# Attention decode with K turned as 32-bit words, column-tiled scores and PV, and fp32 selection matmuls for the outputs

## The chip, the cores and the metric

The kernel runs on one core of a Trainium2 chip. The metric is the device time of that core in microseconds. The profiler's "span" (first to last instruction) is about 1.75 us shorter than that time. TensorE is called PE, VectorE DVE, ScalarE ACT, and the queue that issues the loads SP. A run is called slow when it is over 1.5% above the fastest of the same kernel. A median is over all runs of a kernel, of which one of the changed kernel (127.4 us) and one of a3 (131.91 us) were slow.

## The reference

One decode step for a batch of 8, with attention (32 query heads, 8 key/value heads, a window of 1024 of 4096 positions, head size 128) and a gated feed-forward block beside it.

```python
xn = layernorm(x)                                   # 8 x 512
q  = (xn @ wq)                                      # wq 512 x 4096
k, v = repeat(k_cache[:, :, -1024:, :], 4), repeat(v_cache[:, :, -1024:, :], 4)
p  = softmax(q @ k.T * 128 ** -0.5)
s  = (p @ v).reshape(8, 1, 4096) @ wo               # wo 4096 x 512
g  = silu((gelu(xn @ w_gate) * (xn @ w_up)) @ w_down)   # 512 x 1792, 1792 x 512
out = x + s * g
```

47.46 MB (millions of bytes) have to be read once. In units of 1024 x 1024 bytes, K and V are 32 of it, wq and wo 8, and the feed-forward weights 5.3. Little is computed with each byte.

## The kernel before

The work is cut into 16 groups, each one batch element and four of the eight key/value heads. A group has 1 MB of K and 1 MB of V, one load each. In a K tile partition (n, p) holds 32 positions of head n, each 128 numbers long. PE turns K in 32 pieces of 128 x 128 bf16, DVE copies the turned pieces out of PSUM, 32 small matmuls give the scores (a first product puts -30000 where query and key head differ), ACT takes the exponential, one product with ones gives the row sums, and 32 small matmuls give the outputs.

```python
def load_wq(k):
    t = slot()
    nc.sync.dma_start(out=t, in_=A_wq[k * P : (k + 1) * P, :])
    return t

def turn_k(g, t):                                   # t = 0..3, eight pieces each
    kp = ps_t.tile([P, 8 * P], BF16, name="t_ps")
    for c in range(8):
        r = 8 * t + c
        nc.tensor.transpose(kp[:, c * P : (c + 1) * P], k_t[g][:, r * Dh : (r + 1) * Dh], ident)
    kT = kT_pool.tile([P, 8 * P], BF16, name="kT")
    nc.vector.tensor_copy(out=kT, in_=kp)
    ...
# score(g, t): the mask product (hot x far), then eight 128x128 kT pieces by 16 columns of q
# soft(g): Exp;  values(g): ones x p, 32 pieces of V by 16 columns of p, reduce, reciprocal, multiply

for g in range(NGR + 1):
    ...                                             # issue the loads of V[g], K[g + 2]; at the end the weights
    # turn_k(g, 0..3) interleaved with score(g, 0..2); values(g - 1); score(g, 3); soft(g)
hT = ffn_up()
ffn_down(hT)
...                                                 # 64 products with wo, then s * g + x
```

The softmax here doesn't subtract the row's maximum and nothing guards it: scores larger than these inputs give would overflow.

## Time and profile before

| | before |
|---|---|
| time | 123.04 us, median of three runs (123.03 to 123.2) |
| read from HBM | 47.46 MB |
| PE instructions (matmuls and weight loads) | 1772 + 1772 |
| PE per group at full clock | 4.44 us |
| K and V of a group arrive in | 4.9 us |
| attention ends | 98.5 us |
| last wo load complete | 117.45 us |
| from there to the end of the span | 3.85 us |

From the page of before: busy tenths of the engines in 40 slices of the span, PE's granted clock in tenths, the DMA engines' share and rate, and from the table of DMA queues the instruction fetches (packets, MB, share of 16 engines).

```profile
span 121.3 us, 3885 instructions
PE 96.0 (79%) x1772; PEld 75.6 (62%) x1772; DVE 73.6 (61%) x142; ACT 14.9 (12%) x24; POOL 3.1 (3%) x8
...
PEclk9999955555799999999999999555799955555798
DMA  2999999999999999999999999999999999999820
GB/s 78 394 430 427 427 432 430 416 413 430 424 432 421 430 427 424 408 419 427 432 421 427 419 432 419 421 421 432 430 416 419 419 437 414 416 422 417 343 86 3
...
q8 instruction: 14, 0.23, 0.7%
```

The DMA row is at 9 from the second slice to the 37th: the stream never rests. The last three slices are its ragged end. The windows view of before shows the same; the columns are the stretch in us, its length, busy time (and instructions) of each engine, PE's clock, DMA share and GB/s.

```profile
18.00:24.00 6.00, 6.00 (x85) 4.74 (x83) 3.44 (x6) 1.39 (x2) 0.00 (x0) 0.50 1.02 427
...
114.00:116.00 2.00, 1.09 (x18) 0.87 (x16) 0.00 (x0) 0.00 (x0) 0.00 (x0) 1.00 0.52 207
116.00:118.00 2.00, 1.28 (x17) 0.85 (x15) 0.15 (x1) 0.00 (x0) 0.00 (x0) 1.00 0.20 70
```

The chain of waits of before (start in us, length in us, what it was), first one group of attention in mid-stream, then the end.

```profile
40.99 0.91 PE t_ps L230 x16
41.90 0.32 PE sc_ps L242
...
44.20 0.23 PE a_ps L273
44.43 0.79 PE o_ps L282 x32
...
45.43 0.60 PE t_ps L230 x8
...
101.12 16.03 DMA slot<-in_A_wo_dram
117.15 0.04 issue
117.19 0.64 PE big L469 x8
```

One group takes 45.43 - 40.99 = 4.44 us, half a microsecond less than its data need to arrive, so PE waits for data from 54 us on. Sixteen bf16 transposes take 0.91 us, 57 ns each. At the end PE waits for the last two wo loads (landing at 117.15 and 117.45 us) and has eight products left (L469).

### The profile page before, as it was taken

How to read it: one execution, taken by the hardware profiler on the slowest of the kernel's cores; microseconds unless marked ns; L12 is line 12 of the kernel's file. 1: busy time of each engine (PE TensorE's matmuls, PEld its weight loads, DVE VectorE, ACT ScalarE, POOL GpSimd, SP SyncE). 2: the span in 40 equal slices, each digit the busy share in tenths (PEclk: the TensorE clock that was granted, in tenths of full speed). 3: DMA queues.
4: the chain of work that ended last, by engine and by line, in shares of the span. 5: the costliest groups of instructions: out<-in, count | busy, mean ns of one | idle time of the engine just before them, and what ended most of it. 6: DMA issues, size and time to landing. Idle time of an engine off the chain costs nothing.

```text
span 121.3 us, 3885 instructions
## 1 busy us (share of the span) xinstructions
PE 96.0 (79%) x1772; PEld 75.6 (62%) x1772; DVE 73.6 (61%) x142; ACT 14.9 (12%) x24; POOL 3.1 (3%) x8
## 2 busy tenths in 40 slices
PE   0197269999999999999799993999999783396660
PEld 0192028897787887887778873897888550064540
DVE  4663035475888887888688882665788644704011
ACT  4000043010101101101101101010101103002000
POOL 7200000000000000000000000000000000000000
PEclk9999955555799999999999999555799955555798
DMA  2999999999999999999999999999999999999820
GB/s 78 394 430 427 427 432 430 416 413 430 424 432 421 430 427 424 408 419 427 432 421 427 419 432 419 421 421 432 430 416 419 419 437 414 416 422 417 343 86 3
DMA packets 7392, 47.72 MB, mean 393 GB/s; under 512 B 808, under 2 KB 976, under 8 KB 2768
## 3 DMA queue, kind: packets, MB, share of 16 engines
q1 hardware_dynamic: 7312, 47.46, 93.6%
q8 instruction: 14, 0.23, 0.7%
q10 hardware_dynamic: 64, 0.02, 0.1%
q14 instruction: 2, 0.02, 0.0%
HBM read 47.46 MB, written 0.01 MB: 391 GB/s over the span
## 4 chain that ended last, share of the span: by engine, by line
DMA 56%; PE 34%; DVE 4%; SPq 2%; issue 1%; DVEq 0%
DMA slot<-in_A_k_cache_dram 17%; DMA slot<-in_B_w_up_dram 15%; PE t_ps L230 15%; DMA slot<-in_A_wo_dram 13%; DMA slot<-in_A_wq_dram 10%; PE sc_ps L253 7%; PE o_ps L282 5%; PE sc_ps L242 3%; DVE kT L234 3%; PE a_ps L273 2%; SPq L84 1%; PE t_ps L345 1%; DVE q_sb L340 1%; SPq L89 1%; PE big L469 1%
## 5 line engine op out<-in xcount | busy, mean ns | idle before, releaser
L234 DVE COPY kT<-t_ps 128x1024 bf16<-128x1024 bf16 x64 | 42.6, 690 | 17.4 <-PE t_ps L230 16.6
L230 PE MATMUL t_ps<-ident,slot 128*128 128x128 bf16 x512 | 43.7, 244 | 2.8 <-DMA slot<-in_A_k_cache_dram 2.8
L230 PEld LDWEIGHTS <-slot 128*128 128x128 bf16 x512 | 35.2, 110 | 3.3 <-DMA slot<-in_A_k_cache_dram 3.0
L253 PEld LDWEIGHTS <-kT 128*128 128x128 bf16 x512 | 18.6, 99 | 9.0 <-DVE kT L234 7.3
L253 PE MATMUL sc_ps<-qT_all,kT 128*128 128x16 bf16 x512 | 22.7, 172 | 1.8
L266 ACT ACTIVATE p<-sc_ps 128x512 bf16<-128x512 f32 x16 | 9.6, 597 | 68.1 <-PE sc_ps L253 68.1
L282 PEld LDWEIGHTS <-slot 128*128 128x128 bf16 x512 | 15.7, 98 | 3.5 <-issue 2.2
L282 PE MATMUL o_ps<-p,slot 128*128 128x16 bf16 x512 | 15.7, 171 | 0.0
L290 DVE TENSOR_REDUCE sums<-a_ps 128x16 f32<-128x512 f32 x16 | 11.1, 692 | 1.4 <-PE a_ps L273 1.0
L469 PE MATMUL big<-slot,og 128*64 128x256 bf16 x64 | 5.8, 332 | 2.8 <-DMA slot<-in_A_wo_dram 2.8
L273 PE MATMUL a_ps<-p,ones_pp 128*128 128x512 bf16 x16 | 7.1, 442 | 0.7 <-ACT p L266 0.7
L242 PE MATMUL sc_ps<-far,hot 4*128 4x512 bf16 x16 | 7.3, 453 | 0.0
L469 PEld LDWEIGHTS <-og 128*64 128x64 bf16 x64 | 4.5, 135 | 4.3 <-issue 2.8
L330 PE MATMUL big<-slot,xT 128*32 128x512 bf16 x32 | 3.4, 516 | 3.9 <-DMA slot<-in_A_wq_dram 3.9
L362 PE MATMUL big<-slot,xT 128*32 128x448 bf16 x32 | 3.6, 566 | 2.0 <-DMA slot<-in_B_w_up_dram 2.0
L294 DVE TENSOR_TENSOR oT_all<-o_ps,sums 128x16 bf16<-128x16 f32 x16 | 3.7, 230 | 1.7
L404 PE MATMUL big<-slot,hT 128*32 128x256 bf16 x28 | 3.3, 415 | 1.7 <-DVE hT L389 1.7
L330 PEld LDWEIGHTS <-xT 128*32 128x32 bf16 x32 | 0.9, 104 | 5.8 <-issue 5.7
L340 DVE CAST q_sb<-big 128x512 bf16<-128x512 f32 x1 | 0.7, 692 | 6.2 <-PE big L330 6.2
L293 DVE RECIPROCAL sums<-sums 128x16 f32<-128x16 f32 x16 | 4.0, 253 | 0.5
L480 DVE TENSOR_TENSOR tmp<-big,g_sb 128x256 f32<-128x256 f32 x1 | 0.4, 425 | 6.2 <-PE big L469 6.2
L404 PEld LDWEIGHTS <-hT 128*32 128x32 bf16 x28 | 2.1, 138 | 3.3 <-DVE hT L389 2.5
(50 smaller groups left out, 28.5 us busy)
## 6 DMA issues: line engine op xcount, KB each, us to landing
slot<-in_A_k_cache_dram SPq DMA_DIRECT2D x16, 1024.0 KB, 19.7
slot<-in_A_v_cache_dram SPq DMA_DIRECT2D x16, 1024.0 KB, 20.3
slot<-in_A_wq_dram SPq DMA_DIRECT2D x4, 1024.0 KB, 9.7
slot<-in_A_wo_dram SPq DMA_DIRECT2D x3, 1024.0 KB, 17.7
slot<-in_B_w_gate_dram SPq DMA_DIRECT2D x2, 896.0 KB, 19.4
slot<-in_B_w_up_dram SPq DMA_DIRECT2D x2, 896.0 KB, 18.6
slot<-in_B_w_down_dram SPq DMA_DIRECT2D x2, 896.0 KB
slot<-in_A_wo_dram SPq DMA_DIRECT2D x1, 512.0 KB
```

Of the source, the lines that this page charges most:

```text
L230: nc.tensor.transpose(kp[:, c * P : (c + 1) * P], k_t[g][:, r * Dh : (r + 1) * Dh], ident)
L234: nc.vector.tensor_copy(out=kT, in_=kp)
L242: nc.tensor.matmul(sc.rearrange("p r q -> p (r q)"), hot, far.rearrange("n r q -> n (r q)"), start=True, stop=False, skip_group_check=True,)
L253: nc.tensor.matmul(sc[:, r, :], kT_t[g, t][:, c * P : (c + 1) * P], qT_all[:, i, b, :, :].rearrange("p n j -> p (n j)"), start=False, stop ...
L266: nc.scalar.activation(out=p, in_=sc_t[g], func=ACT.Exp, scale=inv_sqrt_dh)
L273: nc.tensor.matmul(sums_ps.rearrange("p r q -> p (r q)"), ones_pp, p.rearrange("p r q -> p (r q)"), start=True, stop=True,)
L282: nc.tensor.matmul(o_ps, v_t[g][:, r * Dh : (r + 1) * Dh], p[:, r, :], start=(r == 0), stop=(r == NKR - 1),)
L290: nc.vector.tensor_reduce(out=sums, in_=sums_ps.rearrange("p r q -> p q r"), axis=AX.X, op=ALU.add)
L293: nc.vector.reciprocal(out=sums, in_=sums)
L330: nc.tensor.matmul(q_ps[i][32 * j : 32 * j + 32, :], xT[:, 0, k, :], wq_t[k][:, n0 : n0 + 512], start=(k == 0), stop=(k == NDC - 1), tile_ ...
L404: nc.tensor.matmul(f_ps[64 * t : 64 * t + 32, 0:256], hT[:, j, :], w[:, c0 : c0 + 256], start=(j == 0), stop=(j == FR - 1), tile_position= ...
L469: nc.tensor.matmul(s_ps[64 * t : 64 * t + 64, 0:256], og[:, hh, j, :], wo_t[q][:, c0 : c0 + 256], start=(n == 0), stop=(n == len(rows) - 1 ...
```

## The change

The change cuts PE's and DVE's instruction count. K is turned as 32-bit words, two bf16 numbers at a time, so 16 transposes do what 32 did; the scores are then split over even and odd numbers and run as four column tiles of N=512; PV runs as two column tiles of N=512 with P turned on DVE; and the wanted blocks of the PV result are gathered by fp32 products with a selection matrix. The last wq block, one w_down block and the last wo blocks are loaded in smaller pieces, and the residual x is loaded between the wo loads. Cut to its core:

```diff
 def load_wq(k):
     t = slot()
-    nc.sync.dma_start(out=t, in_=A_wq[k * P : (k + 1) * P, :])
+    n = 2 if k == NDC - 1 else 1
+    w = Hq * Dh // n
+    for c in range(0, Hq * Dh, w):
+        nc.sync.dma_start(out=t[:, c : c + w], in_=A_wq[k * P : (k + 1) * P, c : c + w])
 ...
 def turn_k(g, t):
-    for c in range(8):                              # bf16, 128 x 128
+    kw = k_t[g].bitcast(FP32)
+    for c in range(4):                              # words, 128 x 128
+        nc.tensor.transpose(kp[:, c * P : (c + 1) * P], kw[:, rp * P : (rp + 1) * P], ident_f)
-    nc.vector.tensor_copy(out=kT, in_=kp)
+    copy = nc.scalar.copy if t == 1 else nc.vector.tensor_copy
 ...
+    # score(g): mask, even, odd, each as four column tiles of 32 by N=512 (12 products)
+    # soft(g): Exp with row sums;  turn_p(g): 32x32 block transpose of P on DVE
+    # values(g): eight products of N=512 in two column tiles, then ACT copies o_ps to fp32 o_sb
+def gather(g):
+    nc.tensor.matmul(a_ps[:, 0, :], ones_f, ss_t[g], ...)               # fp32
+    for r in range(rep):
+        nc.tensor.matmul(a_ps[:, 1, :], o_t[g][:, r * Dh : (r + 1) * Dh], selr[:, r, :], ...)   # fp32
 ...
+    # Q: four casts (even/odd, twice) and eight copies of 64 partitions, on DVE and ACT in turn
 ...
-parts = [(0, 0, 8), (2, 0, 8), (4, 0, 8), (6, 0, 4), (7, 0, 3), (7, 3, 4)]
+parts = [(0, 0, 8), (2, 0, 8), (4, 0, 8), (6, 0, 4), (7, 0, 2), (7, 2, 3), (7, 3, 4)]
 ...
 for g in range(NGR + 1):
+    # score(g), soft(g), turn_k(g+1, 0), turn_p(g), turn_k(g+1, 1), values(g-1), turn_k(g+1, 2..3), gather(g-1)
```

More of the change, by code (lines that the diff above doesn't have):

```diff
@@ L59 @@
     persist = ctx.enter_context(tc.tile_pool(name="persist", bufs=1))
-    kT_pool = ctx.enter_context(tc.tile_pool(name="kT_pool", bufs=8))
-    p_pool = ctx.enter_context(tc.tile_pool(name="p_pool", bufs=3))
+    kT_pool = ctx.enter_context(tc.tile_pool(name="kT_pool", bufs=2))
+    p_pool = ctx.enter_context(tc.tile_pool(name="p_pool", bufs=2))
+    pT_pool = ctx.enter_context(tc.tile_pool(name="pT_pool", bufs=2))
     small = ctx.enter_context(tc.tile_pool(name="small", bufs=3))
+    o_pool = ctx.enter_context(tc.tile_pool(name="o_pool", bufs=1))
     ffn_sb = ctx.enter_context(tc.tile_pool(name="ffn_sb", bufs=1))
-    ps_t = ctx.enter_context(tc.tile_pool(name="ps_t", bufs=2, space=bass.MemoryType.PSUM))
-    ps_sc = ctx.enter_context(tc.tile_pool(name="ps_sc", bufs=2, space=bass.MemoryType.PSUM))
+    ps_t = ctx.enter_context(tc.tile_pool(name="ps_t", bufs=3, space=bass.MemoryType.PSUM))
+    ps_sc = ctx.enter_context(tc.tile_pool(name="ps_sc", bufs=1, space=bass.MemoryType.PSUM))
     ps_a = ctx.enter_context(tc.tile_pool(name="ps_a", bufs=1, space=bass.MemoryType.PSUM))
@@ L83, in load_wq @@
         t = slot()
-        nc.sync.dma_start(out=t, in_=A_wq[k * P : (k + 1) * P, :])
+        n = 2 if k == NDC - 1 else 1
+        w = Hq * Dh // n
+        for c in range(0, Hq * Dh, w):
+            nc.sync.dma_start(
+                out=t[:, c : c + w], in_=A_wq[k * P : (k + 1) * P, c : c + w]
+            )
         return t
@@ L107, in load_down @@
         n = FR // 2 * D
-        nc.sync.dma_start(
-            out=t[:, 0:n],
-            in_=B_w_down.rearrange("(p j) d -> p (j d)", j=FR)[:, h * n : (h + 1) * n],
-        )
+        rows = B_w_down.rearrange("(p j) d -> p (j d)", j=FR)
+        cut = [0, n] if h == 0 else [0, 4 * D, n]
+        for a, z in zip(cut, cut[1:]):
+            nc.sync.dma_start(out=t[:, a:z], in_=rows[:, h * n + a : h * n + z])
         return t
@@ L137 @@
     k_t[1] = load_kv(A_k_cache, *groups[1])
-    for g in range(NGR):
-        v_t[g] = None
-    stream = []
     ident = consts.tile([P, P], BF16, name="ident")
@@ L153 @@
     )
-    ones_pp = consts.tile([P, P], BF16, name="ones_pp")
-    nc.vector.memset(ones_pp, 1.0)
+    ident_f = consts.tile([P, P], FP32, name="ident_f")
+    nc.vector.tensor_copy(out=ident_f, in_=ident)
+    ones_f = consts.tile([P, P], FP32, name="ones_f")
+    nc.vector.memset(ones_f, 1.0)
     eps_sb = consts.tile([B, 1], FP32, name="eps_sb")
     nc.vector.memset(eps_sb, 1e-5)
-    hot = consts.tile([HN, P], BF16, name="hot")
+    hot = consts.tile([HN, 2, QW], BF16, name="hot")
     nc.vector.memset(hot, 0.0)
     nc.gpsimd.affine_select(
-        out=hot.rearrange("n (p m) -> n p m", m=HN),
-        in_=hot.rearrange("n (p m) -> n p m", m=HN),
+        out=hot.rearrange("n r (m j) -> n r m j", m=HN),
+        in_=hot.rearrange("n r (m j) -> n r m j", m=HN),
         compare_op=ALU.not_equal,
@@ L166 @@
         base=0,
-        pattern=[[0, P // HN], [-1, HN]],
+        pattern=[[0, 2], [-1, HN], [0, rep]],
         channel_multiplier=1,
     )
-    far = consts.tile([HN, NKR, QW], BF16, name="far")
+    far = consts.tile([HN, 512], BF16, name="far")
     nc.vector.memset(far, -30000.0)
     nc.gpsimd.affine_select(
-        out=far.rearrange("n r (m j) -> n r m j", m=HN),
-        in_=far.rearrange("n r (m j) -> n r m j", m=HN),
+        out=far.rearrange("n (c m) -> n c m", m=HN),
+        in_=far.rearrange("n (c m) -> n c m", m=HN),
         compare_op=ALU.not_equal,
@@ L177 @@
         base=0,
-        pattern=[[0, NKR], [-1, HN], [0, rep]],
+        pattern=[[0, 512 // HN], [-1, HN]],
         channel_multiplier=1,
+    )
+    selq = consts.tile([P, QW], FP32, name="selq")
+    nc.vector.tensor_reduce(
+        out=selq,
+        in_=ident.rearrange("p (m q) -> p q m", q=QW),
+        axis=AX.X,
+        op=ALU.add,
+    )
+    selr = consts.tile([P, rep, QW], FP32, name="selr")
+    nc.vector.tensor_reduce(
+        out=selr.rearrange("p r q -> p (r q)"),
+        in_=ident.rearrange("p (u c) -> p c u", u=2),
+        axis=AX.X,
+        op=ALU.add,
     )
@@ L199 @@
     )
-    for t in range(2):
-        nc.scalar.dma_start(
-            out=x_res[64 * t : 64 * t + B, :], in_=x_flat[:, t * 256 : (t + 1) * 256]
-        )
-    xT_ps = ps_t.tile([P, 2, NDC, 32], BF16, name="t_ps")
+    xT_ps = ps_t.tile([P, 2, NDC, 32], BF16, name="t_ps", tag="t")
     for k in range(NDC):
@@ L215 @@
     nc.vector.tensor_copy(out=xT, in_=xT_ps)
-    qT_all = persist.tile([P, NHALF, B, HN, rep], BF16, name="qT_all")
+    q2_all = persist.tile([P, NHALF, B, 2, 2, HN, rep], BF16, name="q2_all")
+    nc.gpsimd.memset(q2_all, 0.0)
     oT_all = persist.tile([P, NHALF, HN, rep, B], BF16, name="oT_all")
-    og = persist.tile([P, Hkv, rep, 64], BF16, name="og")
+    og = persist.tile([P, Hkv * rep + 1, 32], BF16, name="og")
     nc.vector.memset(og, 0.0)
-    kT_t = {}
-    sc_t = {}
-    def turn_k(g, t):
-        kp = ps_t.tile([P, 8 * P], BF16, name="t_ps")
-        for c in range(8):
-            r = 8 * t + c
-            nc.tensor.transpose(
-                kp[:, c * P : (c + 1) * P], k_t[g][:, r * Dh : (r + 1) * Dh], ident
-            )
-        kT = kT_pool.tile([P, 8 * P], BF16, name="kT")
-        nc.vector.tensor_copy(out=kT, in_=kp)
-        kT_t[g, t] = kT
@@ L237, in score, with turn_k @@
-    def score(g, t):
+    wp = persist.tile([P, P, 2], BF16, name="wp")
+    nc.gpsimd.memset(wp, 0.0)
+    nc.gpsimd.memset(wp[:, :, 0], 1.0)
+    wp_ps = ps_t.tile([P, 4 * P], FP32, name="t_ps", tag="t")
+    nc.tensor.transpose(
+        wp_ps[:, 0:P], wp.rearrange("p k e -> p (k e)").bitcast(FP32), ident_f
+    )
+    one = persist.tile([P, 1], FP32, name="one")
+    nc.vector.tensor_copy(out=one, in_=wp_ps.bitcast(BF16)[:, 0:1])
+    kT_t, p_t, pT_t, ss_t, o_t = {}, {}, {}, {}, {}
+    def turn_k(g, t):
+        kp = ps_t.tile([P, 4 * P], FP32, name="t_ps", tag="t")
+        kw = k_t[g].bitcast(FP32)
+        for c in range(4):
+            rp = 4 * t + c
+            nc.tensor.transpose(
+                kp[:, c * P : (c + 1) * P], kw[:, rp * P : (rp + 1) * P], ident_f
+            )
+        if t == 0:
+            kT_t[g] = kT_pool.tile([P, NKR * P], BF16, name="kT")
+        copy = nc.scalar.copy if t == 1 else nc.vector.tensor_copy
+        copy(out=kT_t[g][:, t * 8 * P : (t + 1) * 8 * P], in_=kp.bitcast(BF16))
@@ new lines, with score @@
+    sc_t = {}
+    def score(g):
+        b, i = groups[g]
+        sc = ps_sc.tile([P, 512], FP32, name="sc_ps")
+        sc_t[g] = sc
+        kT = kT_t[g].rearrange("w (r k e) -> w r k e", k=P, e=2)
+        for e in range(-1, 2):
+            for t in range(4):
+                if e < 0:
+                    lhs, rhs = hot.rearrange("n r q -> n (r q)"), far
+                else:
+                    lhs = q2_all[:, i, b, e, :, :, :].rearrange("w r n j -> w (r n j)")
+                    rhs = kT[:, :, 32 * t : 32 * t + 32, e]
+                nc.tensor.matmul(
+                    sc[32 * t : 32 * t + 32, :],
+                    lhs,
+                    rhs,
+                    start=(e < 0),
+                    stop=(e == 1),
+                    skip_group_check=True,
+                    tile_position=(0, 32 * t),
+                )
@@ new lines, in soft, with turn_p @@
+    def soft(g):
+        p = p_pool.tile([P, 512], BF16, name="p")
+        acc = small.tile([P, 1], FP32, name="acc")
+        nc.scalar.activation(
+            out=p, in_=sc_t[g], func=ACT.Exp, scale=inv_sqrt_dh, accum_out=acc
+        )
+        p_t[g] = p, acc
+    def turn_p(g):
+        p, acc = p_t[g]
+        pT = pT_pool.tile([P, 512], BF16, name="pT")
+        nc.vector.transpose(out=pT, in_=p)
+        pT_t[g] = pT
+        ss = small.tile([P, QW], FP32, name="ss")
+        nc.vector.tensor_scalar(
+            out=ss, in0=selq, scalar1=acc[:, 0:1], scalar2=None, op0=ALU.mult
+        )
+        ss_t[g] = ss
@@ new lines, in values @@
+    def values(g):
+        o_ps = ps_o.tile([P, 512], FP32, name="o_ps")
+        for m in range(NKR // 4):
+            u = m % 2
+            nc.tensor.matmul(
+                o_ps[64 * u : 64 * u + 64, :],
+                pT_t[g][:, m * 64 : (m + 1) * 64],
+                v_t[g][:, m * 512 : (m + 1) * 512],
+                start=(m < 2),
+                stop=(m >= NKR // 4 - 2),
+                skip_group_check=True,
+                tile_position=(0, 64 * u),
+            )
+        o_sb = o_pool.tile([P, 512], FP32, name="o_sb")
+        nc.scalar.copy(out=o_sb, in_=o_ps)
+        o_t[g] = o_sb
@@ L238, in score @@
+    def gather(g):
         b, i = groups[g]
-        if t == 0:
-            sc = ps_sc.tile([P, NKR, QW], FP32, name="sc_ps")
-            sc_t[g] = sc
-            nc.tensor.matmul(
-                sc.rearrange("p r q -> p (r q)"),
-                hot,
-                far.rearrange("n r q -> n (r q)"),
-                start=True,
-                stop=False,
+        a_ps = ps_a.tile([P, 2, QW], FP32, name="a_ps", tag="a")
+        nc.tensor.matmul(
+            a_ps[:, 0, :], ones_f, ss_t[g], start=True, stop=True, skip_group_check=True
+        )
+        for r in range(rep):
+            nc.tensor.matmul(
+                a_ps[:, 1, :],
+                o_t[g][:, r * Dh : (r + 1) * Dh],
+                selr[:, r, :],
+                start=(r == 0),
+                stop=(r == rep - 1),
@@ L248, in score @@
                 skip_group_check=True,
             )
-        sc = sc_t[g]
-        for c in range(8):
-            r = 8 * t + c
-            nc.tensor.matmul(
-                sc[:, r, :],
-                kT_t[g, t][:, c * P : (c + 1) * P],
-                qT_all[:, i, b, :, :].rearrange("p n j -> p (n j)"),
-                start=False,
-                stop=True,
-                skip_group_check=True,
-            )
-    p_t = {}
-    def soft(g):
-        p = p_pool.tile([P, NKR, QW], BF16, name="p")
-        nc.scalar.activation(out=p, in_=sc_t[g], func=ACT.Exp, scale=inv_sqrt_dh)
-        p_t[g] = p
@@ L269, in values @@
-    def values(g):
-        b, i = groups[g]
-        p = p_t[g]
-        sums_ps = ps_a.tile([P, NKR, QW], FP32, name="a_ps")
-        nc.tensor.matmul(
-            sums_ps.rearrange("p r q -> p (r q)"),
-            ones_pp,
-            p.rearrange("p r q -> p (r q)"),
-            start=True,
-            stop=True,
-        )
-        o_ps = ps_o.tile([P, QW], FP32, name="o_ps")
-        for r in range(NKR):
-            nc.tensor.matmul(
-                o_ps,
-                v_t[g][:, r * Dh : (r + 1) * Dh],
-                p[:, r, :],
-                start=(r == 0),
-                stop=(r == NKR - 1),
-            )
-        sums = small.tile([P, QW], FP32, name="sums")
-        nc.vector.tensor_reduce(
-            out=sums, in_=sums_ps.rearrange("p r q -> p q r"), axis=AX.X, op=ALU.add
-        )
-        nc.vector.reciprocal(out=sums, in_=sums)
+        rs = small.tile([P, QW], FP32, name="rs")
@@ L294, in values @@
+        nc.vector.reciprocal(out=rs, in_=a_ps[:, 0, :])
         nc.vector.tensor_tensor(
             out=oT_all[:, i, :, :, b],
-            in0=o_ps.rearrange("p (n j) -> p n j", n=HN),
-            in1=sums.rearrange("p (n j) -> p n j", n=HN),
+            in0=a_ps[:, 1, :].rearrange("p (n j) -> p n j", n=HN),
+            in1=rs.rearrange("p (n j) -> p n j", n=HN),
             op=ALU.mult,
@@ L301, in regroup @@
     def regroup(i):
-        rg = ps_a.tile([P, rep, HN, B], FP32, name="a_ps")
+        rg = ps_a.tile([P, rep, HN, B], FP32, name="rg_ps", tag="a")
         sel = ident.rearrange("p (e j) -> p j e", j=rep)
@@ L316, in regroup @@
         nc.vector.tensor_copy(
-            out=og[:, i * HN : (i + 1) * HN, :, 0:B],
+            out=og[:, i * HN * rep : (i + 1) * HN * rep, 0:B].rearrange(
+                "p (h j) b -> p h j b", j=rep
+            ),
             in_=rg.rearrange("p j h b -> p h j b"),
@@ L338 @@
                 )
-    q_sb = persist.tile([P, NHALF, 512], BF16, name="q_sb")
-    nc.vector.tensor_copy(out=q_sb[:, 0, :], in_=q_ps[0])
-    nc.scalar.copy(out=q_sb[:, 1, :], in_=q_ps[1])
+    q_sb = persist.tile([P, NHALF, rep, 2, 2, Dh // 2], BF16, name="q_sb")
     for i in range(NHALF):
-        qT_ps = ps_t.tile([P, rep, HN, 32], BF16, name="t_ps")
-        for c in range(rep):
-            nc.tensor.transpose(
-                qT_ps[:, c, :, :].rearrange("p n b -> p (n b)"),
-                q_sb[:, i, c * Dh : (c + 1) * Dh],
-                ident,
-            )
-        nc.vector.tensor_copy(
-            out=qT_all[:, i, :, :, :].rearrange("p b n c -> p c n b"),
-            in_=qT_ps[:, :, :, 0:B],
-        )
+        for rr in range(2):
+            copy = nc.scalar.copy if rr else nc.vector.tensor_copy
+            copy(
+                out=q_sb[:, i, :, :, rr, :],
+                in_=q_ps[i].rearrange("p (j w e) -> p j e w", j=rep, e=2),
+            )
+    for i in range(NHALF):
+        qT_ps = ps_t.tile([P, rep, 2, HN, 32], BF16, name="t_ps", tag="t")
+        for j in range(rep):
+            for e in range(2):
+                nc.tensor.transpose(
+                    qT_ps[:, j, e, :, :].rearrange("p n b -> p (n b)"),
+                    q_sb[:, i, j, e, :, :].rearrange("p r w -> p (r w)"),
+                    ident,
+                )
+        for e in range(2):
+            for rr in range(2):
+                copy = nc.scalar.copy if rr else nc.vector.tensor_copy
+                copy(
+                    out=q2_all[64 * rr : 64 * rr + 64, i, :, e, rr, :, :].rearrange(
+                        "p b n j -> p j n b"
+                    ),
+                    in_=qT_ps[64 * rr : 64 * rr + 64, :, e, :, 0:B],
+                )
     def ffn_up():
@@ L437 @@
         if g == NGR:
-            parts = [(0, 0, 8), (2, 0, 8), (4, 0, 8), (6, 0, 4), (7, 0, 3), (7, 3, 4)]
-            wo_t = [load_wo(*q) for q in parts]
-        if g < NGR:
-            for t in range(4):
-                if g:
-                    turn_k(g, t)
-                    if t:
-                        score(g, t - 1)
-                elif t:
-                    score(g, t - 1)
+            parts = [(0, 0, 8), (2, 0, 8), (4, 0, 8), (6, 0, 4), (7, 0, 2), (7, 2, 3), (7, 3, 4)]
+            wo_t = [load_wo(*q) for q in parts[:3]]
+            for t in range(2):
+                nc.sync.dma_start(
+                    out=x_res[64 * t : 64 * t + B, :], in_=x_flat[:, t * 256 : (t + 1) * 256]
+                )
+            wo_t += [load_wo(*q) for q in parts[3:]]
+        if g < NGR:
+            score(g)
+            soft(g)
+        if g + 1 < NGR:
+            turn_k(g + 1, 0)
+        if g < NGR:
+            turn_p(g)
+        if g + 1 < NGR:
+            turn_k(g + 1, 1)
         if g:
             values(g - 1)
+        if g + 1 < NGR:
+            turn_k(g + 1, 2)
+            turn_k(g + 1, 3)
+        if g:
+            gather(g - 1)
             if groups[g - 1][0] == B - 1:
                 regroup(groups[g - 1][1])
-        if g < NGR:
-            score(g, 3)
-            soft(g)
+    x_f = persist.tile([P, D // 2], FP32, name="x_f")
     hT = ffn_up()
     ffn_down(hT)
+    nc.vector.tensor_scalar(
+        out=x_f, in0=x_res, scalar1=one[:, 0:1], scalar2=None, op0=ALU.mult
+    )
     s_ps = ps_big.tile([P, 512], FP32, name="big")
@@ L470 @@
                 s_ps[64 * t : 64 * t + 64, 0:256],
-                og[:, hh, j, :],
+                og[:, hh * rep + j : hh * rep + j + 2, :].rearrange("p m b -> p (m b)"),
                 wo_t[q][:, c0 : c0 + 256],
@@ L480 @@
     nc.vector.tensor_tensor(out=tmp, in0=s_ps[:, 0:256], in1=g_sb, op=ALU.mult)
-    nc.vector.tensor_tensor(out=out_sb, in0=tmp, in1=x_res, op=ALU.add)
+    nc.vector.tensor_tensor(out=out_sb, in0=tmp, in1=x_f, op=ALU.add)
     out_flat = out.flatten_outer_dims()
```

## The prediction

> What bounds the kernel. The DMA stream does. The windows view shows a DMA share of 1.00 to 1.04 and 417 to 431 GB/s in nearly every stretch from 6 to 112 us; the page counts 47.46 MB, which at 427 GB/s is 111 us of a 121.3 us span. The rest is a head of 2.3 us before the first packet, a ragged end and 4.1 us after the last landing. The chain of waits names PE for 34%, but PE only keeps up: its group of attention takes 4.4 us at full clock (40.99 to 45.43 in the chain), while a group's K and V (2 MB) take 4.9 us to arrive. PE waits at 54 to 75 us for K, from 98 us for the feed-forward weights and wo. DVE and ACT are further off.
>
> The ragged end is what can be won. The windows show the DMA share falling to 0.52 at 114 to 116 us and 0.20 at 116 to 118. In the trace the sixteen engines finish a load within 0.4 us of each other early, but the last wo loads within 3.1 us. The spread grows by about 1.5 us on one engine each time an instruction fetch (table of DMA queues: 14 packets of 16 KB, about 0.93 us each) falls on it. Fetches come once per 256 PE instructions (3544 in all) and rotate over eight engines, so the ninth begins a second round: five engines are 3 us late, three 1.5 us, the others hardly. The Trainium skill ("DMA: Bandwidth & Descriptors", Queues, rings and completion order) says that each engine takes its queues in turn by packet; the trace agrees.
>
> What the change does, per group. Of 98 matmuls with 98 weight loads it leaves 16 transposes, 12 scores, 8 PV and 5 gathers. I count 1400 to 1750 PE instructions in all, thus 5 to 7 fetches: no engine is hit twice. Costs, estimates: scores as the Q projection (8 column-tiled matmuls of N=512 in 0.62 us at full clock) 0.9 us; PV, two tiles side by side, 1.2; word transposes between one and two times the bf16 ones (16 in 0.91), 0.9 to 1.8; gathers 0.6 to 1.1, as the skill ("FP8 and Floating Point Precision") gives fp32 four passes, which no trace here shows. Sum 3.6 to 5.0 us against 4.4: PE may gain nothing. DVE loses one K copy (0.69) and the reduction (0.69), gains P's transpose (448 columns took 0.98, so 1.1) and a scaling (0.25): even. ACT goes from 0.6 to about 2.3. All below 4.9.
>
> On the critical path: only the fetches' lateness, 3.1 to about 1.6 us. The freed PE time buys nothing. The finer last loads still end with one 128 KB load and two matmuls; the late x adds 8 KB. So about 1.45 us is gained: 121.6 us, range 120.7 to 123.1. Faster by over 2%: 0.15; within 2%: 0.76; slower: 0.09.
>
> What would show it: instruction packets from 14 to 5-7; last wo landing near 115.7 us; DMA rate in mid-stream unchanged; page's LDWEIGHTS down by more than half; 4 us from last landing to end, unchanged.
>
> What would make it wrong: fp32 instructions that are slow or split in several, so that PE's group takes over about 5.1 us, attention ends past 101 us (before: 98.8) and the feed-forward chain of 13 us runs past the stream: each 0.1 us per group then costs 1.6 us. A clock of 0.5, as at 17 to 33 us, would do that too. Nine or more fetches would leave the time unchanged.

## The result, and the profile after

The changed kernel takes 125.19 us (median of four; 124.81, 125.14 and 125.25 fast, 127.4 slow), and the kernel before 123.03 beside it. The ratio of the fast runs is 1.016 (95% interval 1.014 to 1.019). A ratio is always the mean time of one kernel's fast runs over that of the other's of the same rounds, so it is not quite the ratio of the medians quoted. The change is slower by 1.6%, within the 2% that counts as "same", but outside the range of 120.7 to 123.1.

The same lines of after's page:

```profile
span 123.4 us, 2341 instructions
PE 102.1 (83%) x949; PEld 69.5 (56%) x949; DVE 66.7 (54%) x150; ACT 45.1 (37%) x77; POOL 4.2 (3%) x11
...
PEclk9999855555999999999999999999999999778599
DMA  3999899999999999999999999999999999999600
GB/s 69 419 425 427 272 431 425 427 422 427 430 430 430 425 417 427 425 425 422 422 427 427 427 422 430 433 430 419 425 422 423 423 423 416 421 416 411 232 0 3
...
q8 instruction: 7, 0.11, 0.3%
```

PE has 949 matmuls instead of 1772, yet is busy for longer (102.1 against 96.0 us). The fetches are halved. One slice, the fifth, has 272 GB/s where before had 427. The windows view of after:

```profile
12.00:18.00 6.00, 2.13 (x19) 0.71 (x19) 1.13 (x2) 0.59 (x1) 0.00 (x0) 0.69 0.94 350
18.00:24.00 6.00, 4.97 (x35) 3.13 (x33) 3.64 (x7) 3.37 (x6) 0.00 (x0) 0.50 1.01 427
48.00:54.00 6.00, 6.00 (x59) 4.46 (x59) 4.10 (x10) 2.29 (x4) 0.00 (x0) 1.00 1.01 429
...
116.00:118.00 2.00, 2.00 (x34) 1.57 (x30) 0.69 (x2) 0.64 (x2) 0.00 (x0) 0.83 0.16 57
```

PE is busy for 6.00 of 6.00 us in mid-stream, and in the last stretch, where before's PE waited for data, it is working without a pause. The chain of waits of after: its start, one group, its end.

```profile
18.87 0.73 DVE q_all L414
19.62 0.73 ACT q_all L414
...
23.98 1.28 ACT L296
...
28.07 1.04 PE sc_ps L283 x8
...
34.22 0.87 PE sc_ps L283 x11
...
44.07 0.87 PE sc_ps L283 x12
44.94 1.02 PE t_ps L260 x8
45.97 0.98 PE o_ps L317 x8
46.95 1.02 PE t_ps L260 x8
47.97 0.13 PE a_ps L333 x2
48.10 0.89 PE a_ps L337 x8
48.99 0.87 PE sc_ps L283 x12
...
106.56 1.54 PE big L428 x9
...
113.29 3.17 PE big L470 x28
116.46 3.75 PE big L547 x64
120.23 0.44 DVE tmp L558
```

A group takes 48.99 - 44.07 = 4.92 us, and the chain does not leave PE from one group to the next, but for 0.6 us at 68.7 us, between the two halves of the groups. Its parts are scores 0.87, transposes 2 x 1.02, PV 0.98, row sums 0.13, gathers 0.89. The stream brings a group in 4.9 us as well. The scores of group 2 start at 34.2 us, in before at 27.7, and this delay stays to the end: attention ends at 106.2 us instead of 98.5, the feed-forward chain (L428 to L470) follows it, and all 64 products with wo (L547) start only at 116.46 us, when all but the last two wo loads are in.

The ragged end did shrink. The trace holds sixteen landing times of a load, read here as one for each of the sixteen DMA engines (it does not name them). For the last wo load, in us after the first engine, sorted:

```
before  0 .02 .03 .04 .09 .33 .65 .79 1.41 1.43 1.70 2.93 2.94 2.96 3.03 3.10   complete at 117.45
after   0 .04 .06 .08 .10 .41 .54 .55  .97 1.44 1.45 1.46 1.50 1.54 1.54 1.60   complete at 117.08
```

No engine is 3 us late any more. But the load is complete only 0.37 us sooner, because of the slow slice.

The landing times of before tie this to the fetches, load by load. With each fetch one more of the sixteen shares falls about 1.5 us behind, and only after the ninth (73.04 us) is one 3 us behind (3.26 us, in the K load that is complete at 75.06 us). So I infer that the fetches go round eight engines. The thirteen fetches before the last wo load leave five shares about 3 us late and three about 1.5; in after seven fetches leave seven shares 1.4 to 1.6 us late.

So two sums describe the result. The stream's end moved from 117.45 to 117.08 (-0.4 us), and the time from there to the span's end grew from 3.85 to 6.3 us (+2.5): together +2.1 us, as measured.

### The profile page after: what moved, and what is told of

Its sections match the earlier page's. It is cut to its first block, busy times and chain, and to the rows that moved or that the text cites. A ratio compares the mean times of both kernels' runs of the same rounds, so it can differ in the third digit from the quotient of the medians.

```text
span 123.4 us, 2341 instructions
## 1 busy us (share of the span) xinstructions
PE 102.1 (83%) x949; PEld 69.5 (56%) x949; DVE 66.7 (54%) x150; ACT 45.1 (37%) x77; POOL 4.2 (3%) x11
## 4 chain that ended last, share of the span: by engine, by line
PE 70%; DMA 10%; DVE 8%; ACT 6%; SPq 2%; issue 2%; DVEq 0%; ACTq 0%
PE t_ps L260 24%; PE o_ps L317 13%; PE a_ps L337 12%; PE sc_ps L283 11%; DMA slot<-in_A_wq_dram 10%; PE big L547 3%; PE big L470 3%; ACT q_all L414 2%; DVE q_all L414 2%; PE a_ps L333 1%; SPq L89 1%; PE big L428 1%; ACT L296 1%; DVE kT L266 1%; ACT o_sb L327 1%
## 5 line engine op out<-in xcount | busy, mean ns | idle before, releaser
L266 DVE COPY kT<-t_ps 128x1024 bf16<-128x1024 bf16 x48 | 31.8, 688 | 25.4 <-PE t_ps L260 25.4
L260 PE MATMUL t_ps<-ident_f,slot 128*128 128x128 f32 x256 | 38.8, 302 | 0.0
L260 PEld LDWEIGHTS t_ps<-ident_f,slot 128*128 128x128 f32 x256 | 31.3, 154 | 12.7 <-issue 12.6
L266 ACT COPY kT<-t_ps 128x1024 bf16<-128x1024 bf16 x16 | 16.2, 1012 | 9.5 <-PE t_ps L260 9.1
L337 PE MATMUL a_ps<-selr,o_sb 128*128 128x16 f32 x128 | 16.7, 263 | 0.8 <-ACT o_sb L327 0.8
L317 PE MATMUL o_ps<-slot,pT 128*64 128x512 bf16 x128 | 17.0, 388 | 0.0
L337 PEld LDWEIGHTS a_ps<-selr,o_sb 128*128 128x128 f32 x128 | 15.6, 192 | 1.0 <-ACT o_sb L327 1.0
L283 PE MATMUL sc_ps<-kT,q_all 128*32 128x512 bf16 x128 | 10.9, 412 | 2.2 <-DVE kT L266 1.4
L304 DVE STREAM_TRANSPOSE pT<-p 128x512 bf16<-128x512 bf16 x16 | 11.2, 703 | 2.8 <-ACT p L296 2.8
L327 ACT COPY o_sb<-o_ps 128x512 f32<-128x512 f32 x16 | 9.4, 586 | 3.0 <-PE o_ps L317 2.5
L470 PE MATMUL big<-slot,hT 128*32 128x256 bf16 x28 | 3.2, 419 | 3.7 <-DVE hT L455 3.7
L470 PEld LDWEIGHTS <-hT 128*32 128x32 bf16 x28 | 2.0, 144 | 5.2 <-DVE hT L455 4.5
## 6 DMA issues: line engine op xcount, KB each, us to landing
slot<-in_A_wo_dram SPq DMA_DIRECT2D x3, 1024.0 KB, 15.4
```

The source lines that it names most:

```text
L260: nc.tensor.transpose(kp[:, c * P : (c + 1) * P], kw[:, rp * P : (rp + 1) * P], ident_f)
L266: copy(out=kT_t[g][:, t * 8 * P : (t + 1) * 8 * P], in_=kp.bitcast(BF16))
L283: nc.tensor.matmul(sc[32 * t : 32 * t + 32, :], lhs, rhs, start=(e < 0), stop=(e == 1), skip_group_check=True, tile_position=(0, 32 * t),)
L304: nc.vector.transpose(out=pT, in_=p)
L317: nc.tensor.matmul(o_ps[64 * u : 64 * u + 64, :], pT_t[g][:, m * 64 : (m + 1) * 64], v_t[g][:, m * 512 : (m + 1) * 512], start=(m < 2), st ...
L327: nc.scalar.copy(out=o_sb, in_=o_ps)
```

## The experiments

Theory A: in after, PE's chain from the Q projection to the last product sets the time. A group costs PE as much as the stream takes to deliver one, so a late start is never made up. The start is late because of the Q turn, the Exp table and a half clock. The shorter spread comes from fewer instruction fetches, and the slow slice from splitting wq. The rivals are R (the pace of 4.92 is that of K's arrival or of DVE and ACT, not of PE's work), S (the start does not matter, only the pace), and, for the ragged end, that the finer loads and not the fetches shortened it.

All outputs are right. "Ratio" is to the kernel before in the same rounds. The kernel before itself came out at 122.8 to 123.9 us in these rounds, in two clusters: its runs of 123.6 us and more all had a mean clock of 0.846 to 0.850, the faster ones another. Differences of half a microsecond between rounds mean little.

| run | edit | median us | ratio (95%) | last wo complete | expected us |
|---|---|---|---|---|---|
| a1_wq_whole | after, wq block whole | 125.43 | 1.015 (1.008 to 1.022) | 116.06 | 124.0 |
| a2b_gather_bf16 | after, gather in bf16 | 122.26 | 0.991 (0.986 to 0.997) | 117.08 | 122.7 |
| a4_gather_wq | both | 121.56 | 0.984 (0.979 to 0.989) | 116.26 | 121.7 |
| a3_start_early | after, half of the Q turn moved | 130.35 | 1.057 (1.051 to 1.062) | 116.89 | 123.9 |
| a5_warm_exp | after, Exp table early, idle products | 122.74 | 0.995 (0.988 to 1.002) | 117.06 | 122.8 |
| a9_exp_early | after, Exp table early | 123.14 | 0.999 (0.992 to 1.007) | 116.83 | 124.4 |
| a8_all | a4 and a5 together | 121.53 | 0.987 (0.982 to 0.991) | 116.01 | 121.5 |
| a7_more_fetches | a4 with 346 tiny products | 122.75 | 0.996 (0.992 to 1.001) | 117.22 | 122.9 |
| b1_wq_split | before, wq in column halves | 124.5 | 1.010 (1.005 to 1.015) | 118.24 | 124.0 |
| b4_wq_swapped | before, halves in other order | 123.88 | 1.007 (1.000 to 1.014) | 117.71 | 124 |
| b2_wq_rows | before, wq in row halves | 125.11 | 1.015 (1.011 to 1.020) | 119.20 | 123.0 to 123.7 |
| b3_pace | before, 0.5 us more PE work a group | 123.32 | 1.000 (0.994 to 1.005) | 117.42 | 123.0 to 123.5 |

### Is it PE's work per group?

```diff
-o_sb = o_pool.tile([P, 512], FP32, name="o_sb")
+o_sb = o_pool.tile([P, 512], BF16, name="o_sb")
-selr = consts.tile([P, rep, QW], FP32, name="selr")
+selr = consts.tile([P, rep, QW], BF16, name="selr")
```

A first build of this edit failed, as a bf16 reduction has to be allowed explicitly; mended, it is a2b.

> The gather run that did not build, mended: o_sb and the selection matrix in bf16, nothing else. Theory A: about 0.65 us less PE work per group (4.93 to about 4.3), PE catches up with the stream, attention ends near 99 us, the end follows the last wo landing (117.1): about 122.7. Rival R (the pace of 4.93 is that of K's arrival or of DVE/ACT): pace and time unchanged, 125.1.

It took 122.26 us. Rival R falls: with the same K copies on DVE and ACT and the same loads, 0.65 us less of PE work per group gave back 2.9 us of the median. The pace went only to 4.6 us, not 4.3, because PE then waits for DVE's K copies (below); that was enough, and attention ended at 101.1 us.

```diff
 # a4: a2b and
-n = 2 if k == NDC - 1 else 1
+n = 1
```

> The same, and the last wq block loaded whole. Alone that moved nothing, as PE's chain set the end; here the stream should set it, so its microsecond should show: last wo landing 116.0, about 121.7, faster than both kernels. If the stream is not what ends the chain once PE has caught up: no better than the gather run.

121.56 us, the fastest so far and faster than both kernels. The chain of waits of a4, a group and the end:

```profile
39.08 0.62 PE sc_ps L284 x6
39.70 1.04 PE t_ps L261 x8
40.74 0.98 PE o_ps L318 x8
41.72 0.60 PE t_ps L261 x4
...
42.35 1.30 DVE kT L267 x2
...
43.69 0.62 PE sc_ps L284 x8
...
104.11 10.87 DMA slot<-in_A_wo_dram
...
116.31 0.31 PE big L548 x2
```

A group takes 43.69 - 39.08 = 4.61 us and now holds a wait for DVE. At the end the chain is the DMA's again, with two products after the last load, as in before.

### Does the late start matter, and by itself?

```diff
 # a3: Exp table early, as in a9, and
-for i in range(NHALF):          # casts, transposes and copies of both halves of Q
+turn_q(0)                       # the first half; turn_q(1) in iteration 1, before turn_k(2, 1)
```

> After, with the Exp table loaded at about 4 us instead of at 24 us in front of the first Exp, and the second half of the Q turn (i=1: two casts, eight transposes, four copies, needed only from group 8) moved into iteration 1. Theory A (late start never made up): first Exp at 22.5 instead of 25.3, score of group 1 about 1.2 us earlier, all later groups and the end as much earlier: about 123.9. Rival S (groups run at the stream's pace, the start does not matter): the last group's scores stay at 99.2 us and the time at 125.1.

This was meant to start earlier and did the opposite. The second half of the Q turn landed in the middle of a group, where its two casts and four copies, one after another, held up the K copies. In its trace (a slow run; the other three took 129.9 to 130.8) the scores of group 2 start at 38.2 us instead of 34.2, PE's clock is at 0.5 until 44.7 us except from 34.5 to 37.9, and the next group starts at 46.1 instead of 39.1. The end came 4.8 us later (129.94 against 125.14, the medians of the fast runs). As an edit it was a mistake; as evidence it speaks against S: an early delay of 4 to 7 us stayed to the end.

```diff
 # a5
+nc.scalar.activation(out=warm, in_=rstd, func=ACT.Exp)     # loads the Exp table at about 4 us
 for k in range(NDC):
+    if k >= 2:
+        keep_busy(24)                                      # 24 products of N=128, never read
```

> After at its own pace of 4.93 us per group, but with an earlier start: the Exp table loaded at about 4 us instead of 24, and 24 idle matmuls (their result is not read) before each of the last two wq blocks, so that the clock is not throttled to 0.5 at 14.6 us. Theory A (the start is never made up): score of group 2 starts at about 31.8 us instead of 34.2, the end comes 2.4 us earlier until the last landing (117.1) limits it: about 122.8. Rival S (only the pace matters): 125.1. If the clock falls to 0.5 all the same, about 1.2 us are gained: 123.9.

122.74 us, with the pace untouched: the start alone gave back 2.4 us by the medians. In the trace (123.24 us) group 2 starts at 32.3 us instead of 34.2, attention ends at 104.4, and the span is shorter by the same 1.9 us. The idle products did less than expected: they held the clock at 1.0 until 19.3 us instead of 14.3, but it was 0.5 from there to 29.5.

```profile
32.30 0.87 PE sc_ps L285 x12
```

> After, with only the Exp table loaded early (by a one-column Exp at about 4 us), clock left alone: parts the 2.4 us that table and clock gave together. The first Exp goes from 25.3 to about 24.0 us, but the last K copies of group 1 then end at about 27.3 instead of 28.0, as their transposes run at the half clock until 26.1. So I expect about 0.8 us: 124.4. If the table was all of it: 122.8. If only the clock mattered: 125.1.

With the table alone (the first line of a5's edit) the median was 123.14, but the four runs fall apart: 122.39, 122.46, 123.81 and 124.10. The traced one is the slowest; its group 2 starts 1.1 us earlier than in after and its end is 1.0 us earlier, near the 0.8 expected. The two fast ones have no trace, so how table and clock share the gain stays open.

```diff
 # b3: before
+for _ in range(9):
+    nc.tensor.matmul(sums[:, 0:P], ident, ident, start=True, stop=True)   # overwritten next
```

> Before, with nine idle products of 57 ns per group in front of the row sums, so that its PE needs about 4.95 us per group, as after's does, but starts as before (scores of group 0 at 18.3 us). If late start and lost slack together make after slow, the pace alone costs little: attention ends near 101.5 us, the stream still ends the kernel, 123.0 to 123.5. If the pace of 4.93 by itself makes after slow: 125.

123.32 us, ratio 1.000. The group took 94.65 - 89.68 = 4.97 us by the chain of waits, as slow as in after, and attention still ended at 99 us. So the pace of 4.9 is harmless where the start is early.

```profile
89.68 0.52 PE a_ps L274 x9
...
94.65 0.52 PE a_ps L274 x9
```

In this trace the clock was back at 1.0 at 23.3 us (before: 31.6). That helped it (group 2 starts at 26.9 us, in before at 27.6), and it was not the edit's doing, as the first added product runs at 24.2. All four runs lie between 122.9 and 123.7, but the other three have no trace. So this pace behind the whole of before's half clock is not shown.

```diff
 # a8: a4's two edits and a5's two edits
```

> Gather in bf16, wq whole, and also the Exp table early and the clock kept up. Theory A: once PE's group has slack (4.6 us against 4.9), the start is made up anyway and the stream sets the end, so the earlier start gains nothing: 121.5, last landing 116.2. Rival: the start still counts by 2 us, as it did in the run at 4.93 us per group: under 120.5.

121.53 us against 121.56. Once the group has slack, the earlier start is worth nothing, as expected.

### The slow slice: the split of wq

The edit of a1 is the second one of a4 alone.

> After, with the last wq block loaded whole (1 MB) instead of in two column halves. Theory A (TensorE's chain from the Q projection to the end sets the time; a group costs PE 4.93 us, the stream brings one in 4.91 us, so a late start is never made up; and the split cost the stream about 1 us, because the first half ran at some 230 GB/s): wq complete at 15.8 us instead of 16.9, every group about 1.1 us earlier, last wo landing 116.0 instead of 117.1, time about 124.0. Rival (the dip at 12.5 to 14.6 us was chance, or has nothing to do with the split): wq and last landing unmoved, 125.1, or the dip shows again.

Half of this was wrong. The slow slice vanished (426 GB/s from 12 to 18 us, after 350) and the last wo load was complete at 116.06 instead of 117.08 us. But the time stayed, at 125.43 (three runs at 125.3 to 125.6; a fourth, without a trace, took 123.91, and why is not known). The expectation overlooked that the first half of Q needs only the first half of the split block: it started at 15.7 us in after and at 15.8 with the whole block. PE's chain was as long as ever, so a stream faster by 1 us was worth nothing. That is the plainest evidence that the stream does not end after.

> Before, with the last wq block loaded in two column halves as after does it. If the split slows the stream by about 1 us, the last wo landing goes from 117.4 to about 118.4 and, as this kernel's end follows that landing, the time from 123.0 to about 124.0. If the dip in after's trace was chance: 123.0.

With the split (the first hunk of the change, put into before) the kernel before is slower by 1.0%, and the slice reappears (355 GB/s from 12 to 18 us). The last wo load was complete 0.8 us later (118.24 instead of 117.45). The traced run's span is longer by 1.9 us, though: the other 1.1 us lie after that load, where the clock is 0.5 (in before 1.0) and the chain ends with 32 products of wo in 3.64 us. So the stream's loss shows in the landing, and the 1.0% is not all its doing.

```diff
 # b2: before, the last wq block by rows
-nc.sync.dma_start(out=t, in_=A_wq[k * P : (k + 1) * P, :])
+for p in range(0, P, P // 2):
+    nc.sync.dma_start(out=t[p : p + P // 2, :], in_=A_wq[k * P + p : k * P + p + P // 2, :])
```

> Before, with the last wq block in two loads by rows (64 partitions each, whole rows of 8 KB) instead of by columns (half rows of 4 KB at a stride of 8 KB). If the stream lost its microsecond to the half rows: no dip at 12.5 to 14.6 us, time as before (123.0 to 123.7, as before beside it). If to the fact of two loads: the dip again, 1 us slower.

It was slower still, by 1.5%, and both halves ran at half rate: 209 GB/s in the mean from 13.4 to 17.4 us, a packet of 8 KB taking about 0.62 us instead of 0.31. This was not the control it was meant to be. The Trainium skill ("SBUF — State Buffer", Door 1: The DMA port swizzle) says that partitions 0 to 63 reach only 8 of the 16 DMA ports, and so do 64 to 127; half the rate is what the run shows. It says nothing of half rows.

```diff
 # b4: b1's split, with
-for c in range(0, Hq * Dh, w):
+for c in reversed(range(0, Hq * Dh, w)):
```

> Before, with the last wq block in two column halves, the second half loaded first. If whichever half is issued first is slow (it comes after whole rows, or it opens the rows): the dip again at 12.5 to 14.6 us, 1 us slower, 124. If it is the first half's addresses: the dip moves to the second load, at 14.1 to 16 us. If neither: no dip.

The half that is issued first is slow again (205 to 253 GB/s from 13.3 to 14.5 us), whichever columns it holds; the second runs at about 430. So it is not the addresses of the first half. Pieces of 4 KB are not slow as such: the second half has them too. Why the first load of half rows is slow remains open. By the rate from 12 to 18 us (350 to 384 GB/s instead of 426) the column split costs 0.6 to 1.1 us of stream in all seven traces that have it; that is my estimate. The last landing moved by less in b4: 117.71 us instead of 117.45.

### The ragged end: the fetches

```diff
 # a7: a4, in score(g) before its first product
+for _ in range(16):
+    nc.tensor.matmul(sc[0:32, 0:32], ident[:, 0:32], ident[:, 0:32], ...)   # overwritten next
 # and after ffn_up()
+for _ in range(90): ...                                                      # the same, into a free bank
```

> The run with gather in bf16 and wq whole (121.56), plus 346 tiny idle products (about 20 ns a pair at full clock; 16 per group where PE waits for DVE's K copies, 90 where PE waits for the gelu chain). They add 692 PE instructions, so that a ninth instruction fetch comes at about 104 us, while PE's chain keeps its slack. Fetch theory (a fetch delays one engine by 1.5 us, they rotate over eight engines, the ninth falls on an engine that had one): the spread of the last wo landing goes from 1.8 to about 3.1 us, the last landing from 116.3 to about 117.6, the time to about 122.9. Rival (the finer last loads or the late x gained the early landing, not the fetches): spread and time as without, 121.6.

122.75 us, 1.2 us slower than a4, with the same loads in the same pieces. The last wo load's engines were spread over 2.83 us (a4: 1.83), one of them alone at the end, the next at 1.71. The load was complete 0.96 us later than in a4, and the time from there to the end was the same (3.61 and 3.68 us). The table of queues of a7:

```profile
q8 instruction: 9, 0.15, 0.4%
```

Instructions that cost PE next to nothing cost the kernel a microsecond, because the ninth fetch, as its one late share says, fell on a DMA engine that already had one. The rival (finer loads or the late x) falls: a7 has both, and the spread is nearly before's. The Trainium skill ("Runtime: NRT & Kernel Launch", Instruction fetch mechanics) says that each engine's instructions are refilled in blocks of 16 KiB (256 instructions) and that the cost is "mostly hidden". The traces agree with the block: fetches come about every 256 PE instructions. The cost is hidden from PE (in after a group with a fetch in it, at 42.88 us, took 4.93 us, and one without 4.92), but not from a stream that keeps all sixteen engines full.

## Why the prediction was wrong

- **Right: the fetches and the spread.** Expected were 5 to 7 fetches and a lateness of 1.6 us instead of 3.1; measured, 7 and 1.60. Weight loads fell by "more than half" only nearly (1772 to 949). PE instructions were 1898, above the 1400 to 1750 counted: each of the 80 fp32 products is two matmuls and two weight loads.
- **Right: "The freed PE time buys nothing."** PE gained none. Of the parts, scores (0.9 expected, 0.87 measured), PV (1.2, 0.98) and gathers (0.6 to 1.1, 1.02 with the row sums) were sized well. The word transposes were put at "between one and two times the bf16 ones" and take 2.04 us a group: 1.02 us for eight is 128 ns each, 2.2 times the 57 ns of bf16. Half as many words at over twice the price cost more than before. The sum, 4.92, was at the upper end of the stated 3.6 to 5.0.
- **Wrong: "so that PE's group takes over about 5.1 us" as the limit of harm.** This is the step that failed. As its words read ("each 0.1 us per group then costs 1.6 us"), it took 16 groups at a steady pace from before's start, 18.2 us. In after the scores of group 0 start at 19.9 us and the first two groups take 34.2 - 19.9 = 14.3 us; in before they take 27.6 - 18.2 = 9.4. The half clock is in both (to 31.3 and 31.6 us), so it is what after does under it that differs: by the chain the Q copies, the Exp table and the word transposes. Their shares were not measured, but for the 1.9 us that table and clock gave in a5's trace. From the scores of group 2 (34.2 us) there are 13 groups to those of group 15 and 7.0 us to the end of attention (99.2 to 106.2). To end attention at 100.4 us, as a4 does, a group may take (100.4 - 7.0 - 34.2) / 13 = 4.55 us: an estimate of mine, and a4 does it with 4.6, as its last part is shorter (6.0 us). The kernel's 4.92 was inside the limit as predicted and outside the limit as it was. The prediction named the danger, a late feed-forward chain and a clock of 0.5, but gave it 9 chances in 100.
- **Wrong: "On the critical path: only the fetches' lateness".** The Q turn was read as a change of layout, and its four casts and eight copies, one after another between DVE and ACT from 16.4 to 23.9 us, were not costed at all. They and the Exp table behind them belong to PE's chain. a5 moved the table and part of the clock and got back 2.4 us.
- **Wrong: the last landing "near 115.7 us".** It was 117.08. The finer loads were taken to be free, but the split of wq cost 1.0 us (a1: 116.06 without it).
- **Wrong: "4 us from last landing to end, unchanged".** It became 6.3, because 64 products with wo waited for PE. With PE in time it is 3.7 (a4: 116.26 to 119.94).
- **The gain that was predicted exists.** With the gather in bf16 and wq whole the kernel takes 121.56 us, where 121.6 had been predicted for the change itself. The mechanism of the gain was right; what swallowed it was a PE chain with no slack behind a late start. That the two agree to 0.1 us is partly luck: a4's last landing is later than predicted (116.26 instead of 115.7) and the time after it shorter (3.7 instead of 4).

## What to carry to other kernels

Where a stream bounds a kernel, ask not only whether each engine's work per step fits under the stream's step, but by how much: the difference is all it has to make up a late start, and a kernel with none carries the first microseconds' delay to the end. Judge a "cheaper" instruction by its time and not by its number, since here the 32-bit transposes (2.04 us a group instead of 1.82) cost more than their count saved, and the fp32 gathers 3.7 times what they cost in bf16. When the stream is full to the brim, count what else uses its engines, instruction fetches too, and try each split of a load by itself before trusting it.

## What the Trainium skill lacked or had wrong

- "TensorE: Matmul & The Clock Gate" (Terms) calls the transpose mode 4 times faster for FP32 but gives no time for it; the times on the page are for bf16. Here a 128 x 128 transpose of fp32 words took 128 ns against 57 ns in bf16, at full clock and back to back.
- "FP8 and Floating Point Precision" (TensorE Precision Notes) gives true fp32 four passes. The trace shows two weight loads and two matmuls for each fp32 product; four gathers took 0.89 us in fp32 and 0.24 in bf16, a ratio of 3.7.
- "Runtime: NRT & Kernel Launch" (Instruction fetch mechanics) calls the cost of a refill "mostly hidden". Under a full stream each 16 KB fetch made one share of the later loads about 1.5 us late, and only the ninth fell on a share that was late already: 13 fetches before the last load spread it over 3.1 us, 7 over 1.6 to 1.8, 9 over 2.8.
- "TensorE: Matmul & The Clock Gate" (Part 1) has the clock released after one busy window of about 3.4 us. In before the clock stayed at 0.5 from 14.6 to 31.6 us, five such windows, though the profile counts PE as busy for 6.00 of 6.00 us from 18 to 24. This does not prove the page wrong: its Part 4 says that transposes do not count as busy in the same way, and they were 3.46 of the 6.19 us of the group from 19.75 us on. In b3 the clock was back at 23.3 us, before its edit first ran (24.2 us), so the length also differs between runs of the same work.
- No page that I found says that a 1 MB load split into two column halves can lose rate: from 12.6 to 14.6 us, in the first half, the rate was 236 to 289 GB/s in the seven traces with the split, then 432 to 453 (15.4 to 17.4 us), and the split cost 0.6 to 1.1 us. The cause is open.
